# B and C of pairs 4 to 11 turned by the DMA crossbar instead of by PE and two evacuations

**Chip, cores, metric.** One core of a Trainium2 chip. The metric is the device time of one launch in microseconds (us). Engines: PE is TensorE (PEld its weight loads), DVE VectorE, ACT ScalarE, POOL GpSimd, SP SyncE, which here only issues DMAs.

## The reference, cut to what matters

A chunked state-space layer feeds a gated feed-forward layer. Cut:

```python
# x (4, 8, 768, 32), a (4, 8, 768), B and C (4, 8, 768, 16); float32
for c in range(nc):                       # chunks of 32 in the reference
    CB = einsum('bhin,bhjn->bhij', Cc, Bc)          # needs B and C with n on the contracted axis
    y_intra = einsum('bhij,bhjd->bhid', CB * L, xc)
    y_inter = einsum('bhin,bhnd->bhid', Cc, state) * decay_to_i
    state = decay_full * state + sum_j(Bc xc decay_from_j)
# then, per token: (relu(y @ w_gate) * (y @ w_val)) @ w_out, widths 256, 1536, 256
```

Tokens arrive on the partitions. The kernel's matmuls contract over the partitions, so B and C have to be turned before CB and y_inter; the state needs B unturned.

## The kernel before: the parts that matter

Work is cut into 12 pairs of 128-token chunks and 6 blocks of 512 tokens of the feed-forward layer. Block b carries the attention work of P = 2b+2 and Q = 2b+3 between its matmuls. The kernel keeps each engine's instructions in program order (its helper `in_order`). `inter(p)` is the first PE work that reads CT, `G(p)` the first that reads BT; `fout` is the feed-forward layer's last product.

```python
def transp(p, k, apart=False):                     # PE, into PSUM
    ...
    for i in range(2):
        nc.tensor.transpose(out=s["tp"][k][:, i], in_=s["tin"][k][i], identity=ident)

def tevac(p, beng, ceng):                          # BT: one copy; CT: two masked copies
    ...
    (beng.copy if beng is nc.scalar else beng.tensor_copy)(rows(BT), tokens(0))
    if ceng is nc.scalar:
        for t in range(2):
            nc.scalar.mul(rows(CT[:, t]), tokens(1), tmask[:, t:t + 1])
        return
    ...
for b in range(NBLK):
    P, Q, W = 2 * b + 2, 2 * b + 3, 2 * b + 1
    more = P < NPAIR
    for n in (P + 2, P + 3):                       # loads for the NEXT block, twelve DMAs on SP
        if n < NPAIR:
            load(n, nc.sync, nc.sync, nc.sync)
    ...                                            # gvh of f = 0..3; inter, Dm, yevac of W
    for f in range(4, NF):
        gv(b, f)
        if at("scale P", 4, 4, 4): scale(P, nc.gpsimd, nc.gpsimd)
        ...
        if at("turn P", 7, 6, 5):
            turn(P); tevac(P, nc.scalar, nc.vector)
        if at("turn Q", 99, 9, 8):
            turn(Q); tevac(Q, nc.scalar, nc.scalar)
    if more:
        inter(P, 0); inter(P, 1)                   # first reader of CT
    fout(b, 0); foevac(b, 0)
    if more:
        G(P); gevac(P)
    ...                                            # fout 1 and 2, Dm(P), G(Q), fout 3; outputs on SP
```

## Time and profile before

| | before |
|---|---|
| time | 135.2 us (135.13 to 136.19, 3 runs) |
| profiled run (136.74 us) | span 134.9 us, mean clock 0.987 |
| PE busy | 125.1 us (93%) |
| the 32 PE transposes that go | 0.22 us per four on the chain |

In the table of groups (line, engine, operation, tiles, shapes, count, busy us, mean ns of one, idle time before them) these are the ones that the change removes in part:

```profile
L318 PE MATMUL tp<-ident,bs 128*128 128x128 bf16 x44 | 4.4, 219 | 0.0
...
L338 ACT COPY BT<-tp 128x256 bf16<-128x256 bf16 x10 | 3.8, 376 | 0.5
...
L341 ACT ACTIVATE CT<-tp,tmask 128x256 bf16<-128x256 bf16 x8 | 3.4, 479 | 0.0
```

One PE transpose has a duration of 219 ns, but in a row they are pipelined: four advance the chain by 0.22 us. The chain, not the duration, is what a removed instruction gives back. The other lines of this profile are in the prediction.

### The profile page before, as it was taken

What the parts mean: (1) busy time and instruction counts of PE and PEld (TensorE: products, weight loads), DVE (VectorE), ACT (ScalarE), POOL (GpSimd) and SP (SyncE); (2) the same over time, 40 slices, a digit from 0 to 9 for tenths busy, and PEclk for the clock granted to TensorE, in tenths of its full rate; (3) what the DMA queues carried; (4) which work ended last, traced back from release to release, by engine and by line L of the source; (5) the groups of instructions that cost most, each with busy time, mean ns of one, the idle gap of its engine ahead of it and who ended that gap; (6) DMA issues with size and microseconds to landing.
All of it is one profiled execution on the core that took longest, in us unless ns stands there. A gap on an engine that the chain in (4) does not pass through costs nothing.

```text
span 134.9 us, 3130 instructions
## 1 busy us (share of the span) xinstructions
PE 125.1 (93%) x1150; PEld 82.7 (61%) x1157; DVE 90.7 (67%) x195; ACT 81.9 (61%) x177; POOL 37.8 (28%) x76
## 2 busy tenths in 40 slices
PE   6995398999999999999999999999999999999990
PEld 2444156555878656778557786567785577864780
DVE  5796086778637897657867568965588675687611
ACT  4075066547477776468784478764687845887410
POOL 7066063720209200248000293002480002200000
PEclk9999869999999999999999999999999999999999
DMA  3999999999423699028991239780220002200022
GB/s 70 190 151 192 211 187 135 201 190 104 44 78 96 77 119 102 3 83 149 121 114 10 78 87 120 90 99 3 83 78 0 0 0 83 78 0 0 5 80 76
DMA packets 68991, 12.10 MB, mean 90 GB/s; under 512 B 62768, under 2 KB 68976, under 8 KB 68976
## 3 DMA queue, kind: packets, MB, share of 16 engines
q1 hardware_dynamic: 62896, 8.88, 44.2%
q0 software_dynamic: 3184, 2.36, 11.7%
q10 hardware_dynamic: 2896, 0.66, 2.7%
q8 instruction: 9, 0.15, 0.5%
q14 instruction: 6, 0.05, 0.1%
HBM read 11.11 MB, written 3.15 MB: 106 GB/s over the span
## 4 chain that ended last, share of the span: by engine, by line
PE 57%; DVE 1%; issue 0%; DVEq 0%
PE o L490 19%; PE val L463 11%; PE gv L478 11%; PE gate L460 10%; PE y L435 2%; PE g L361 2%; PE A_ps L398 1%; PE tp L318 1%; PE y L424 1%; DVE h L467 0%; DVE ob L503 0%; DVEq L503 0%
## 5 line engine op out<-in xcount | busy, mean ns | idle before, releaser
L467 DVE TENSOR_TENSOR h<-r,val 128x512 bf16<-128x512 bf16 x48 | 32.6, 686 | 9.7 <-ACT r L466 8.8
L490 PE MATMUL o<-wo,h 128*128 128x256 bf16 x288 | 35.0, 273 | 0.1
L466 ACT ACTIVATE r<-gate 128x512 bf16<-128x512 f32 x48 | 28.3, 601 | 8.5 <-PE gate L460 6.2
L369 POOL TENSOR_SCALAR_AFFINE_SELECT gs<-gs 128x512 bf16<-128x512 bf16 (+1 forms) x24 | 12.4, 540 | 69.7 <-ACT gs L380 69.7
L490 PEld LDWEIGHTS <-h 128*128 128x128 bf16 x288 | 27.4, 98 | 5.1 <-issue 1.3
L463 PE MATMUL val<-yT,wv 128*128 128x512 bf16 x96 | 28.6, 379 | 0.3
L460 PE MATMUL gate<-yT,wg 128*128 128x512 bf16 x90 | 27.3, 379 | 0.3 <-ACT r L466 0.3
L482 DVE TENSOR_TENSOR h<-r,gv 128x256 bf16<-128x256 bf16 x48 | 20.0, 421 | 11.1 <-ACT r L481 10.5
L386 DVE TENSOR_TENSOR gs<-g,maskUT 128x512 bf16<-128x512 f32 x24 | 15.4, 686 | 12.9 <-issue 11.8
L481 ACT ACTIVATE r<-gv 128x256 bf16<-128x256 f32 x48 | 18.5, 385 | 6.6 <-PE gv L478 5.1
L478 PE MATMUL gv<-yT,wg 128*128 128x256 bf16 x96 | 18.8, 279 | 2.0 <-DMA wg<-in_moe_w_gate_dram 1.5
L478 PE MATMUL gv<-yT,wv 128*128 128x256 bf16 x96 | 19.0, 281 | 1.6 <-DMA wv<-in_moe_w_val_dram 1.6
L463 PEld LDWEIGHTS <-wv 128*128 128x128 bf16 x96 | 9.4, 98 | 11.3
L460 PEld LDWEIGHTS <-wg 128*128 128x128 bf16 x96 | 8.9, 98 | 7.1 <-issue 0.5
L380 ACT CAST gs<-g 128x512 bf16<-128x512 f32 x12 | 7.1, 589 | 9.2 <-PE g L361 9.0
L448 ACT CAST yT<-y 128x512 bf16<-128x512 f32 x12 | 7.0, 586 | 8.1 <-PE y L435 6.7
L478 PEld LDWEIGHTS <-wg 128*128 128x128 bf16 x96 | 9.1, 99 | 4.3 <-DMA wg<-in_moe_w_gate_dram 1.7
L478 PEld LDWEIGHTS <-wv 128*128 128x128 bf16 x96 | 9.5, 100 | 3.2 <-DMA wv<-in_moe_w_val_dram 1.9
L264 POOL TENSOR_TENSOR bs<-bcr,scaleBC 128x256 bf16<-128x256 f32 x16 | 9.6, 624 | 0.0
L506 ACT COPY ob<-o 128x512 f32<-128x512 f32 x10 | 5.9, 586 | 4.7 <-PE o L490 4.7
L406 DVE TENSOR_TENSOR Sm<-A_ps,smask 128x256 bf16<-128x256 f32 x20 | 8.3, 417 | 0.0
L163 PE MATMUL w<-warm 128*128 128x512 bf16 x18 | 6.2, 491 | 1.4 <-DVE bcr L81 1.3
(75 smaller groups left out, 110.8 us busy)
## 6 DMA issues: line engine op xcount, KB each, us to landing
out_dram<-ob SPq DMA_DIRECT2D x10, 256.0 KB, 2.2
xr<-in_x_dram SPq DMA_DIRECT2D x17, 128.0 KB, 3.8
bcr<-in_B_dram SPq DMA_DIRECT2D x16, 64.0 KB, 3.6
bcr<-in_C_dram SPq DMA_DIRECT2D x16, 64.0 KB, 3.4
xr<-in_x_dram SPq DMA_DIRECT2D x3, 256.0 KB, 7.3
wg<-in_moe_w_gate_dram POOLq DMA_DIRECT2D x3, 256.0 KB, 6.2
wv<-in_moe_w_val_dram POOLq DMA_DIRECT2D x3, 256.0 KB, 7.3
wo<-in_moe_w_out_dram POOLq DMA_DIRECT2D x1, 768.0 KB, 9.5
```

The source lines that it names most:

```text
L264: eng.tensor_tensor(out=bs.rearrange("s k (q t n) -> s k t q n", q=4, t=2)[:, :, t], in0=src[:, :, t], in1=f[:, :, 4 * t:4 * t + 4].to_bro ...
L369: nc.gpsimd.affine_select(out=dst, in_=dst, pattern=[[0, n], [1, 128]], compare_op=ALU.is_ge, fill=0.0, base=0, channel_multiplier=-1)
L386: nc.vector.tensor_tensor(out=d[:, q], in0=g[q], in1=m, op=ALU.mult)
L406: nc.vector.tensor_tensor(out=n, in0=A_ps, in1=smask, op=ALU.mult)
L460: nc.tensor.matmul(out=g, lhsT=wg[:, k, fs], rhs=yT[:, k, tk], start=(k == 0), stop=(k == 1))
L463: nc.tensor.matmul(out=v, lhsT=wv[:, k, fs], rhs=yT[:, k, tk], start=(k == 0), stop=(k == 1))
L466: nc.scalar.activation(r, g, AF.Relu)
L467: nc.vector.tensor_tensor(out=fst[b][:, f], in0=r, in1=v, op=ALU.mult)
L478: nc.tensor.matmul(out=gv_[:, j], lhsT=w[:, k, fs], rhs=yT[:, k, tk], start=(k == 0), stop=(k == 1), skip_group_check=True)
L481: nc.scalar.activation(r, gv_[:, 0], AF.Relu)
L482: nc.vector.tensor_tensor(out=fst[b][:, f, u * 256:(u + 1) * 256], in0=r, in1=gv_[:, 1], op=ALU.mult)
L490: nc.tensor.matmul(out=o[:, ts % 2], lhsT=fst[b][:, f, ts * 128:(ts + 1) * 128], rhs=wo[:, f], start=(f == 0), stop=(f == NF - 1), skip_gr ...
```

## The change

Intent: PE is the bound, so take the turns off it, and off ACT and DVE which empty them. POOL writes B and C, scaled, into a token-major tile with C in two copies that have zeros in the other half's columns (so no masking is needed later); one DMA through the crossbar (`dma_start_transpose`, which transposes on the way) turns all six 128x128 squares into SBUF.

```diff
+    def scale_turn(p):
+        ...
+        w = bc[p % NBC]                       # 3 buffers of [128, 6, 128], zeroed once
+        for j in range(2):
+            for t in range(2):
+                k = 2 * (1 + t) if j else 0
+                nc.gpsimd.tensor_tensor(out=w[:, k:k + 2]...[:, :, t], in0=..., in1=..., op=ALU.mult)
+        T = att.tile([128, 6, 128], BF16, tag="T", name="T")
+        nc.sync.dma_start_transpose(out=T, in_=w.rearrange("s k r -> s (k r)"))
+        s["B"] = [w[:, i] for i in range(2)]
+        s["BT"] = T[:, 0:2]
+        s["CT"] = T[:, 2:6].rearrange("r (t i) m -> r t i m", t=2)
+        cast_x(p, nc.gpsimd)
 ...
+            if b > 0 and more and f == 4:
+                scale_turn(P)
+                scale_turn(Q)
-            if at("turn P", 7, 6, 5):
+            if b == 0 and f == 7:
                 turn(P)
                 tevac(P, nc.scalar, nc.vector)
 ...
-            if at("turn Q", 99, 9, 8):
-                turn(Q)
-                tevac(Q, nc.scalar, nc.scalar)
```

Cut: the zeroing of `bc` on POOL in block 0, and the conditions that keep block 0 as it was. The loads stay at the head of each block.

More of the change, by code (lines that the diff above doesn't have):

```diff
@@ L251, in scale @@
         cast_x(p, ceng)
+    NBC = 3
+    bc = [const.tile([128, 6, 128], BF16, name="bc%d" % k) for k in range(NBC)]
+    def scale_turn(p):
+        b, c0 = p // PPB, 2 * (p % PPB)
+        s = st[p]
+        w = bc[p % NBC]
+        f = scaleBC[:, b, c0:c0 + 2].rearrange("s c j h -> s c (j h)")
+        for j in range(2):
+            for t in range(2):
+                k = 2 * (1 + t) if j else 0
+                nc.gpsimd.tensor_tensor(
+                    out=w[:, k:k + 2].rearrange("s i (q t n) -> s i t q n", q=4, t=2)[:, :, t],
+                    in0=s["bcr"][:, :, j, 4 * t:4 * t + 4],
+                    in1=f[:, :, 8 * j + 4 * t:8 * j + 4 * t + 4].to_broadcast([128, 2, 4, N]),
+                    op=ALU.mult)
+        T = att.tile([128, 6, 128], BF16, tag="T", name="T")
[4 more added lines that the diff above has]
+        cast_x(p, nc.gpsimd)
     def scale_bc(p, eng):
@@ L582 @@
                 decay()
-            if at("scale P", 4, 4, 4):
+            if b == 0 and f == 6:
+                for w in bc:
+                    nc.gpsimd.memset(w, 0.0)
+            if b == 0 and f == 4:
                 scale(P, nc.gpsimd, nc.gpsimd)
-            if at("scale Q", 8, 5, 4):
+            if b == 0 and f == 8:
                 scale(Q, nc.gpsimd, nc.gpsimd)
-            if at("turn P", 7, 6, 5):
+            if b > 0 and more and f == 4:
+                scale_turn(P)
+                scale_turn(Q)
+            if b == 0 and f == 7:
                 turn(P)
```

## The prediction

> **What bounds the kernel now.** I read the page's first two parts, then the chain that ended last in order of time, then the groups by line, then the issues of the sync engine's DMA queue (SP) as a timeline, then the table of stretches with the DMA share.
>
> ```profile
> PE 125.1 (93%) x1150; PEld 82.7 (61%) x1157; DVE 90.7 (67%) x195; ACT 81.9 (61%) x177; POOL 37.8 (28%) x76
> ...
> PE   6995398999999999999999999999999999999990
> ...
> PEclk9999869999999999999999999999999999999999
> ```
>
> TensorE (PE) is busy 93% of the span; from slice 7 (about 24 us) on every slice is full. A busy PE need not be the bound, so the chain is asked next. From 53.5 us on it is PE alone, piece touching piece, until the last evacuation. Here is the end of block 2 (b=2), from its second turn on:
>
> ```profile
> 68.52 0.22 PE tp L318 x4
> 68.74 0.43 PE gate L460 x2
> 69.17 0.43 PE val L463 x2
> 69.61 0.11 PE A_ps L398
> 69.71 0.43 PE gate L460 x2
> 70.15 0.43 PE val L463 x2
> 70.58 0.43 PE gate L460 x2
> 71.01 0.43 PE val L463 x2
> 71.44 0.11 PE y L424 x2
> 71.55 1.41 PE o L490 x12
> ```
>
> The columns are start, length, what. A turn of one pair (four transposes, L318) takes 0.22 us of this chain and nothing waits for it. The y piece of L424 is the first reader of CT on PE: `inter(P)`. So PE in program order is the bound, the other engines have slack, and the only direct gain is PE time.
>
> **What the Trainium skill says.** (1) "VectorE: DVE Perf Modes", section "The three transpose paths": a 128x128 bf16 transpose is given as 390 ns on TensorE and 1309 ns by the DMA crossbar, the latter into SBUF. This trace has 219 ns for one PE transpose and, in a row, 0.22 us for four; it has no crossbar transfer. (2) "Advanced Engine Details and Errata", section "X-Bar Transpose (TRN2)": such DMAs are said to be as fast as regular ones. That contradicts (1) for one of 196 KB unless (1) is nearly all fixed cost; no run yet tells. (3) "DMA: Bandwidth & Descriptors", section "Queues, rings and completion order": on each DMA engine the descriptors of one issuer's ring are consumed in order, so a transfer issued last starts last. The trace agrees as far as it goes: SP issues in program order and the last of a burst of loads lands when the burst has drained. (4) "TensorE: Matmul & The Clock Gate", section "Part 1": about 3.4 us of idleness halves the PE clock, and about as much work restores it. The trace agrees: PE is nearly idle from 13 to 16 us, then the granted clock is 0.50 in three successive stretches of 1 us and 0.83 in the next.
>
> **The change part by part.**
>
> *Removed on PE.* Pairs 4 to 11 lose their turns: 8 x 4 transposes. In the chain each turn is 0.22 us, so 8 x 0.22 = 1.76 us, 0.44 us in each of blocks 1 to 4. The end follows in full, if nothing else waits: 135.2 - 1.8 = 133.4 us.
>
> *Removed on ACT and DVE.* BT copies of pairs 4 to 11: 8 x 375 ns; CT of the P pairs on DVE: 4 x 685 ns; CT of the Q pairs on ACT: 8 x 479 ns. That is 6.8 us of ACT and 2.7 us of DVE, none of it on the chain. PE was held by ACT in the gate group for 0.3 us in all, so I count 0.
>
> *Added on POOL.* Each pair has four multiplies of 128x128 in place of two of 128x256 (624 ns). Taking the length to grow with the elements plus a small fixed part, I estimate 360 ns each, so 1.44 us for 1.25 us per pair. POOL idles for 10 us per block (its causal masks wait 69.7 us in total for ACT), so 0. The three memsets of the padded tiles, estimated at 0.85 us each from the 568 ns of the 128x512 memset, fall between the two scales of block 0: the second scale ended at 27.9 us and would end at about 30.4, and its turn comes at 35.1. Again 0.
>
> *Moved, and this decides it.* The turned C is now ready when a DMA lands. The instruction order of the changed kernel on SP has, in each of blocks 1, 2 and 3: twelve loads for the next block, then the transpose of P, the transpose of Q, then the outputs. POOL has its inputs scaled early (about 4 us after the block's start), but the transposes stand in the SP queue behind loads that are not needed until the next block. When does SP get there? In the kernel before, the twelve loads of block 2 are these (start and length of issue, first and last):
>
> ```profile
> 60.83 0.42 SPq L109 DMA_DIRECT2D xr<-in_x_dram  x1
> ...
> 68.87 0.58 SPq L111 DMA_DIRECT2D bcr<-in_C_dram  x1
> ```
>
> They cannot start earlier, because the outputs of the block before stand ahead of them and wait for ACT. The last issue ends at 69.45 us, where `inter(P)` starts at 71.44. And the rings are still full then (columns: stretch, length, busy time and count of PE, PEld, DVE, ACT and POOL, the clock, the DMA share, GB/s):
>
> ```profile
> 69.00:70.00 1.00, 1.00 (x7) 0.51 (x6) 0.44 (x1) 1.00 (x4) 0.00 (x0) 1.00 1.20 134
> 70.00:71.00 1.00, 1.00 (x6) 0.47 (x5) 0.59 (x1) 0.87 (x2) 0.00 (x0) 1.00 1.44 103
> 71.00:72.00 1.00, 1.00 (x11) 0.76 (x9) 1.00 (x4) 0.60 (x1) 0.00 (x0) 1.00 0.08 6
> ```
>
> The loads drain at about 71.1 us. The same views give a last issue at 52.2 and a drain near 53.9 in block 1, and 89.3 and 91.0 in block 3. Counted from the blocks' starts (first gv piece at 40.8, 59.7 and 78.3), the drains are at 13.1, 11.4 and 12.7 us. `inter(P)` stood at 11.7 and comes at 11.3 without the two turns. So PE is already waiting by 1.8, 0.1 and 1.4 us (3.3 us in all) when the first byte of the transpose can move; then come the transfer and its completion.
>
> How long is that? The tile is 128x768 bf16, 196 KB, six squares. Three estimates. As a regular DMA: the 256 KB outputs land 2.2 us after issue, so about 2 us. By (1), scaled by six: 7.9 us, surely too much if part of the 1309 ns is fixed. By short pieces: the loads move 1024 runs of 64 or 128 bytes each, one load per 0.72 us or so; a transpose that must write runs of 32 bytes would write 6144 and so take some 4 us. I choose 3.5 us after the drain. The stall is then 3.3 + 3 x 3.5 = 13.8 us in blocks 1 to 3. Block 4 has no loads: its transposes go out when POOL is done, about 3 to 5 us into the block, with 7 us in hand, so 0 there.
>
> *The clock.* A stall of 3.5 to 5.3 us idles PE long enough for the clock to fall, in some blocks and not in all. At half speed for about 3.2 us, as at 16 to 19 us, PE loses 1.6 us; I count 3 us for the three blocks.
>
> *Q.* Its transpose follows P's by one transfer. `G(Q)` comes 5.0 us after `inter(P)` (76.47 less 71.44), which covers any transfer under 5 us: 0.
>
> *Sum.* 135.2 - 1.8 + 13.8 + 3 = 150.2, so 150 us, 11% slower.
>
> **The rivals.** *Hidden transfer:* the loads leave earlier or the crossbar overtakes them, nothing waits, and 133.4 us results, "same" by the 2% rule and a little better in truth. For it: POOL could feed the transpose 7 us ahead of need, and DMA is idle in half of the slices. Against it: the SP order, and the drain times above, at or after the need even with a transfer of zero length. *Fast crossbar:* 2 us after the drain, stalls of 3.8, 2.1 and 3.4 us, little or no loss of clock, so about 143 to 145 us. *Slow crossbar:* 7.9 us each. Then P stalls by 3.3 + 23.7 = 27 us, Q adds up to 3 us a block (less where PE is at half clock), and the clock costs 5 us: 166 to 174 us. A slow issue on SP would look the same. *Relief of ACT or DVE as a gain beyond PE's:* the chain has no such waits to give back, so under 0.5 us.
>
> **Range and chances.** Most weight lies between the fast crossbar and some way towards the slow one: 141 to 164. To be within 2% the three stalls together must stay under 4.5 us, while 3.3 us of that is there before a byte moves; I give this 6%. To be over 2% faster needs more than the whole PE saving, 2%. Slower: 92%.
>
> **What would show it.** If right, the chain of the profile after holds three waits of PE on the DMA of T, of 3 to 6 us, ahead of y of L424 (its line is moved by 25 in the changed file) in blocks 1, 2 and 3, and none in block 4, whose length shrinks by about 0.44 us; SP shows the transposes after the twelfth load; the granted clock dips to about 0.5 after at least one stall; blocks 0 and 5 keep their lengths. If the transposes are issued right at POOL's end, or PE waits nowhere for T, the central step is wrong. If the waits are there but of another length, the size of the crossbar's time is what failed. Waits ahead of `G(Q)` would mean a transfer of over 5 us.

## The result, and the profile after

The changed kernel takes 143.3 us (median of 4 runs, 141.32 to 144.17), the kernel before in the same rounds 135.28 us (135.13 to 136.19). A ratio here is the mean time of one kernel's fast runs over that of the other's of the same rounds, so not quite the ratio of the medians: 1.0529, interval 1.041 to 1.0648. Slower by 5%, where 11% was forecast.

The profiled run is the slowest (144.17 us) and counts as slow, being over 1.5% above the fastest. So what is read from it is checked below against runs of equal clock. From its page: PE's busy time and, in 40 slices, PE and the granted clock.

```profile
PE 126.7 (89%) x1118; PEld 82.6 (58%) x1125; DVE 88.8 (62%) x191; ACT 76.7 (54%) x161; POOL 41.9 (29%) x95
...
PE   6999689999999946999995999955999999999990
...
PEclk9999869999999996899999999999999999999999
```

PE was full from slice 7 on; now it has three holes, and the clock dips once after the first of them. What the holes wait for, from PE's rows of the waits (engine, line, releaser: us in total, times, longest) and PE's timeline (start, length, what, and idle time before it):

```profile
PE y L449 <- DMA T<-bc: 8.2, 3, 3.2
```

```profile
54.75 0.61 PE L449 MATMUL y<-T,Sm 128*128 128x128 bf16 x4 [3.23 <-DMA T<-bc]
...
76.48 0.28 PE L449 MATMUL y<-T,Sm 128*128 128x128 bf16 x2 [1.96 <-DMA T<-bc]
...
97.62 0.40 PE L449 MATMUL y<-T,Sm 128*128 128x128 bf16 x4 [3.01 <-DMA T<-bc]
```

Exactly three waits, all at `inter(P)`, in blocks 1, 2 and 3; block 4 has none. The SP queue's timeline shows why T is late. In each block the last of twelve loads and the transposes behind it:

```profile
50.61 0.58 SPq L111 DMA_DIRECT2D bcr<-in_C_dram  x1
51.29 2.83 SPq L272 DMA_TRANSPOSE T<-bc  x2
...
72.52 1.00 SPq L111 DMA_DIRECT2D bcr<-in_C_dram  x1
73.62 2.56 SPq L272 DMA_TRANSPOSE T<-bc  x2
...
92.59 2.11 SPq L111 DMA_DIRECT2D bcr<-in_C_dram  x1
94.81 2.58 SPq L272 DMA_TRANSPOSE T<-bc  x2
```

P's transpose lands 3.4, 2.8 and 2.8 us after SP takes it up, and PE's reader starts within 0.05 us of that. POOL is not late: in this trace its multiplies for P and Q are through at 44.0, 67.1 and 87.2 us, 6.5 to 7.6 us before SP takes the transposes up. The dip, in stretches of 1 us (stretch, length, busy us and count of PE, PEld, DVE, ACT and POOL, the clock, DMA share, GB/s):

```profile
54.00:55.00 1.00, 0.25 (x3) 0.26 (x4) 0.00 (x0) 0.00 (x0) 0.00 (x0) 0.82 0.89 173
55.00:56.00 1.00, 1.00 (x8) 0.76 (x6) 0.00 (x0) 0.00 (x0) 0.00 (x0) 0.50 0.12 24
56.00:57.00 1.00, 1.00 (x6) 0.75 (x5) 0.00 (x0) 0.00 (x0) 0.00 (x0) 0.50 0.00 0
57.00:58.00 1.00, 1.00 (x9) 0.45 (x11) 0.00 (x0) 0.00 (x0) 0.00 (x0) 0.50 0.00 0
58.00:59.00 1.00, 1.00 (x15) 0.68 (x8) 0.52 (x1) 0.59 (x2) 0.00 (x0) 0.97 0.00 0
```

A trace cut into blocks is the cleanest comparison, since the start of a run varies. Block lengths in us, from the first `gvh` matmul of one block to that of the next (the last to the span's end, so to 0.1 us), each from the profiled run's PE timeline:

| kernel | 0 | 1 | 2 | 3 | 4 | 5 |
|---|---|---|---|---|---|---|
| before | 26.61 | 18.78 | 18.61 | 18.51 | 18.40 | 19.9 |
| changed | 26.54 | 23.01 | 20.19 | 21.25 | 17.95 | 20.0 |
| e1, transposes first | 25.48 | 18.07 | 18.06 | 18.07 | 17.95 | 20.1 |
| e2, no turn at all | 27.01 | 18.06 | 18.06 | 18.07 | 17.95 | 19.9 |

Block 4 of the changed kernel is 0.45 us shorter than before, the other three are longer.

### The profile page after: what moved, and what is told of

Read it like the earlier page. It is cut to its first block, busy times and chain, and to the rows that moved or that the text cites. A ratio compares the mean times of both kernels' runs of the same rounds, so it can differ in the third digit from the quotient of the medians.

```text
span 142.5 us, 3079 instructions
## 1 busy us (share of the span) xinstructions
PE 126.7 (89%) x1118; PEld 82.6 (58%) x1125; DVE 88.8 (62%) x191; ACT 76.7 (54%) x161; POOL 41.9 (29%) x95
## 3 DMA queue, kind: packets, MB, share of 16 engines
q0 software_dynamic: 3184, 2.36, 11.4%
## 4 chain that ended last, share of the span: by engine, by line
PE 50%; SPq 19%; DMA 17%; issue 5%; ACT 3%; DVE 2%; POOL 1%; ACTq 0%; DVEq 0%; POOLq 0%
PE o L515 19%; SPq L111 14%; PE gv L503 8%; PE val L488 7%; PE gate L485 7%; DMA T<-bc 6%; SPq L109 5%; DMA wv<-in_moe_w_val_dram 4%; DMA bcr<-in_B_dram 4%; DMA out_dram<-ob 2%; PE g L386 2%; PE y L460 2%; PE y L449 2%; DVE gs L411 1%; PE A_ps L423 1%
## 5 line engine op out<-in xcount | busy, mean ns | idle before, releaser
L515 PE MATMUL o<-wo,h 128*128 128x256 bf16 x288 | 36.0, 279 | 0.0
L491 ACT ACTIVATE r<-gate 128x512 bf16<-128x512 f32 x48 | 28.7, 599 | 12.2 <-PE gate L485 11.2
L515 PEld LDWEIGHTS <-h 128*128 128x128 bf16 x288 | 28.1, 100 | 5.0 <-issue 1.3
L266 POOL TENSOR_TENSOR bc<-bcr,scaleBC 128x128 bf16<-128x128 f32 x32 | 11.9, 403 | 0.0
L449 PE MATMUL y<-T,Sm 128*128 128x128 bf16 x28 | 3.1, 232 | 8.2 <-DMA T<-bc 8.2
L449 PEld LDWEIGHTS <-Sm 128*128 128x128 bf16 x40 | 3.2, 107 | 10.5 <-DMA T<-bc 9.7
```

Of the source, the lines that this page charges most:

```text
L266: nc.gpsimd.tensor_tensor(out=w[:, k:k + 2].rearrange("s i (q t n) -> s i t q n", q=4, t=2)[:, :, t], in0=s["bcr"][:, :, j, 4 * t:4 * t + ...
L491: nc.scalar.activation(r, g, AF.Relu)
L515: nc.tensor.matmul(out=o[:, ts % 2], lhsT=fst[b][:, f, ts * 128:(ts + 1) * 128], rhs=wo[:, f], start=(f == 0), stop=(f == NF - 1), skip_gr ...
```

## The experiments

The theory (A): the transposes stand in SP's queue behind twelve loads that nobody needs before the next block. Rivals: (B) the crossbar transfer, or its traffic, is itself the cost wherever it stands; (C) POOL makes its input late. Then the two sizes, of the transfer and of the clock's dip, were asked.

**e1: the loads behind the transposes.**

```diff
-        for n in (P + 2, P + 3): ...load(n, ...)          # at the head of every block
+        if b == 0: (the same)                             # block 0 alone
 ...
             if b > 0 and more and f == 4:
                 scale_turn(P)
                 scale_turn(Q)
+                for n in (P + 2, P + 3): ...load(n, ...)
```

> The changed kernel with one move: in blocks 1 to 3 the twelve loads for the next block are issued after the two crossbar transposes and no longer before them. Theory A (the transposes stand in the sync engine's queue behind loads that nobody needs yet): no wait of PE on T in any block, no dip of the clock after block 0, 133.0 to 134.0 us (before less 1.76 us of PE time). Rival B (the crossbar transfer or its traffic beside PE and the loads is itself what costs): the waits on T stay at over 1 us each in blocks 1 to 3 and the time stays above 138 us. Rival C (POOL makes the transposes' input late): as B, with SP seen waiting for POOL up to the need of T.

Measured: correct, 133.62 us (133.25 to 134.98), ratio to before 0.9885 (0.9812 to 0.9957). No wait on T. SP in block 2 of this kernel, and PE's first reader of T there:

```profile
58.14 0.38 SPq L532 DMA_DIRECT2D out_dram<-ob  x1
59.41 3.20 SPq L272 DMA_TRANSPOSE T<-bc  x2
62.67 0.57 SPq L109 DMA_DIRECT2D xr<-in_x_dram  x1
...
72.59 3.99 SPq L532 DMA_DIRECT2D out_dram<-ob  x2
```

```profile
68.61 0.28 PE L449 MATMUL y<-T,Sm 128*128 128x128 bf16 x2
```

The reader has no idle time before it and starts 6 us after both transposes are issued. The same instructions and the same bytes, in another order on one queue, take the whole loss away. B and C both fall.

**e2: no turn at all** (a wrong result on purpose).

```diff
-        T = att.tile([128, 6, 128], BF16, tag="T", name="T")
-        nc.sync.dma_start_transpose(out=T, in_=w.rearrange("s k r -> s (k r)"))
+        T = Tfix                                          # one zeroed tile for all
```

> Wrong result on purpose: the transposes are left out and one zeroed tile stands in for every T, so that the turned operands cost nothing at all. It measures the removed work alone. If the removed PE time is the only gain: 133.0 to 134.0 us (135.3 less 1.76), blocks 1 to 4 shorter by 0.44 us each. If the relief of ACT and DVE, or fewer waits elsewhere, were worth more: under 132.8 us. If the saving is taken back by another wait of PE: over 134.5 us.

Measured: wrong as meant, 134.2 us (133.0 to 135.39, 16 runs), ratio 0.9861 (0.9833 to 0.989). Its blocks 1 to 4 are those of e1 to 0.01 us (table above): once its order is right, the crossbar costs nothing in these blocks, and e1 has the whole gain that this change can give. The sum of the four savings is 2.16 us, where 1.76 was forecast; blocks 3 and 4 give the 0.44 us each, blocks 1 and 2 give 0.72 and 0.55.

**e3: only Q by the crossbar**, P by PE as before, loads still first.

```diff
             if b > 0 and more and f == 4:
-                scale_turn(P)
+                scale(P, nc.gpsimd, nc.gpsimd)
                 scale_turn(Q)
+            if b > 0 and at("turn P", 7, 6, 5):
+                turn(P); tevac(P, nc.scalar, nc.vector)
```

> The changed kernel with P's turn back on PE (and its two evacuations) in all blocks; only the Q pairs go through the crossbar, still behind the loads. G(Q) comes 5 us after inter(P). Theory A: a T that lands some 3 us after the loads' last issue is in time for Q, so no wait on T, half of the PE saving: 134.2 to 134.8 us. Rival B (crossbar traffic itself disturbs): a wait of PE on T of over 1 us per block, or other instructions lengthened, over 136 us.

Measured: correct, 134.57 us (133.48 to 135.73, 20 runs), ratio 0.9893 (0.9863 to 0.9922), no wait of PE on T. The very position in the queue that makes P late is in time for Q, whose first reader `G(Q)` stands 5 us further down PE's program: T landed 2.1, 2.9 and 1.9 us before it in blocks 1 to 3. So not the transposes' place alone but place against deadline counts.

**e4: the transposes on ACT's queue**, loads unchanged on SP.

```diff
-        nc.sync.dma_start_transpose(out=T, in_=...)
+        nc.scalar.dma_start_transpose(out=T, in_=...)
```

> The changed kernel with the two transposes issued from ACT's queue, in ACT's program order after the relu of f=4, the loads unchanged on SP. The DMA engines are as full of load traffic as before, but the transposes no longer stand behind all twelve loads in issue. Theory A (order of issue is what counts): T lands about 8 us into the block, no wait on T, 133.2 to 135 us, the upper end if each issue holds ACT for over a microsecond. Rival B (the 16 DMA engines, filled by loads, are the bound, whoever issues): T lands at about the same time as in the changed kernel and the time stays over 140 us.

Measured: correct, 138.67 us (137.72 to 140.11), ratio 1.0201 (1.0136 to 1.0265). There is no wait on T, so A stands here as well: among full load traffic it landed 4.8 us (median) after its issue and that was early enough. But the time missed the forecast by nearly 4 us. ACT's and PE's timelines in block 1:

```profile
44.13 2.69 ACTq L272 DMA_TRANSPOSE T<-bc  x2
46.92 1.57 ACT L491 ACTIVATE r<-gate 128x512 bf16<-128x512 f32 x3 [2.25 <-PE gate L485]
```

```profile
47.56 0.59 PE L488 MATMUL val<-yT,wv 128*128 128x512 bf16 x2 [0.94 <-ACT r L491]
```

The two issues hold ACT for 2.7 us. The relu that would free a PSUM bank comes late, and PE waits in each of the four blocks: PE's waits for this relu are 3.5 us in all, of the 4.2 us by which blocks 1 to 4 are longer than e1's; the rest is not accounted for. (The wait's label on the relu says PE; the relu's operand had long been there, and what ended its idle time was ACT's own queue.) An issue of a transpose is not free for the engine that does it.

**e5: dummy matmuls in the stall.**

```diff
         if more:
+            if 1 <= b <= 3:
+                keep_warm(9)                              # 9 matmuls of 512 columns
             inter(P, 0)
```

> The changed kernel with nine dummy matmuls of 512 columns (9 x 0.216 = 1.9 us of PE time at full clock) on PE just before inter(P) in blocks 1 to 3, where PE otherwise waits 3.2, 2.0 and 3.0 us for T. If the three waits are set by T's landing alone, the dummies fit into them: the end does not move later, the remaining waits shrink to about 1.3, 0 to 0.2 and 1.1 us, and the clock is never halved in them; so every run sits where the changed kernel's run of clock 1.000 sits, 141 to 142 us, about 1 to 1.5 us under the changed kernel's median. If T were not what PE waits for (or the dip of the clock were only a bystander), the dummies would add up to 3 x 1.9 us: 145 to 149 us.

Measured: correct, 143.71 us (142.15 to 144.75), ratio 1.0483 (1.0403 to 1.0563), against the changed kernel's 1.0529. The waits on T shrank from 8.2 to 3.5 us while 5.8 us of work was put in, and in the profiled run the clock stayed at 1.000, block 1 falling from 23.01 to 21.59 us. So most of the dummies fit into the stall, as A says. But the end did not come earlier, as I had expected: blocks 2 and 3 became 0.3 and 0.7 us longer. T landed 3.0 and 3.5 us after its issue there and not 2.8 and 2.8, and in block 2 its issue came 0.2 us later too. The two runs at a clock of 1.000, 142.15 and 142.88 us, lie above the changed kernel's one such run, 141.32. The verdict on the whole time is inconclusive.

**e6: useful work in the stall.**

```diff
+        fout(b, 0)
         if more:
             inter(P, 0)
             inter(P, 1)
-        fout(b, 0)
```

> The changed kernel with fout(b,0), 12 matmuls worth 1.31 us, moved from behind inter(P) to ahead of it, so that useful work stands in the stall; loads and transposes stay in their order. Theory A (three waits for a T that lands at a fixed time): each wait shrinks by 1.3 us, no dip, total about 143.3 - 3 x 1.3 - 1 = 138 to 139 us. Rival (the loss is not in these waits but spread, by traffic or by a slower clock): no gain to speak of, 142 to 144 us.

Measured: correct, 140.06 us (138.68 to 144.06, 5 runs), ratio 1.0318 (1.0242 to 1.0394): 2.1 points below the changed kernel, less than the 3 to 4 expected. The waits are still 2.1, 1.4 and 2.4 us: in the profiled runs T landed 0.2, 0.8 and 0.7 us later in its block than in the changed kernel, and 1.31 us less these is what each wait shrank by. The profiled run (a slow one) shows a halved clock at the end of the wait of 2.1 us in block 1:

```profile
55.00:56.00 1.00, 0.00 (x0) 0.00 (x0) 0.00 (x0) 0.00 (x0) 0.00 (x0) 1.00 1.09 164
56.00:57.00 1.00, 0.04 (x1) 0.04 (x2) 0.00 (x0) 0.00 (x0) 0.00 (x0) 0.94 0.64 125
57.00:58.00 1.00, 1.00 (x12) 0.44 (x12) 0.00 (x0) 0.00 (x0) 0.00 (x0) 0.50 0.77 147
```

**e7: each transpose cut in two**, C's four squares, then B's two.

```diff
-        nc.sync.dma_start_transpose(out=T, in_=w...)
+        for k0, k1 in ((2, 6), (0, 2)):
+            nc.sync.dma_start_transpose(out=T[:, k0:k1], in_=w[:, k0:k1]...)
```

> The changed kernel with each transpose cut in two: the four squares of C first (inter(P) needs only these), then the two of B. It measures how the crossbar's time depends on size. If the 1.22 us that SP spends on one transpose is proportional to its size and the rest of the 2.8 us to landing is fixed, C takes 0.8 us of SP and lands after 2.4 us, B takes 0.4: each of the three waits shrinks by 0.4 us and the time is 1 to 1.5 us below the changed kernel, 142 us. If the time to landing is fixed whatever the size: no change of the first wait, landing at 2.7 us, within 0.5 us of the changed kernel. If it is the data that takes the time behind the loads (my forecast, 3.5 us after the drain for 196 KB): waits shorter by a third, over 1 us each, under 140.5 us.

Measured: correct, 146.23 us (141.79 to 146.66); one run is fast, three are slow with a mean clock of 0.962, so there is no ratio. It answers the question of size. The transposes of the changed kernel (SP's time for one, min/median/max in ns; then us from issue to landing), and of e7:

```profile
L272 SPq DMA_TRANSPOSE T<-bc x8: 1211/1223/1503, 51.3 to 108.5; - x8
...
DMA to landing us min/median/max: 2.7/2.8/3.5
```

```profile
L273 SPq DMA_TRANSPOSE T<-bc x16: 1189/1239/1637, 51.0 to 112.8; - x16
...
DMA to landing us min/median/max: 2.3/2.4/4.1
```

SP spends 1.2 us on a transpose of two, four or six squares alike. The twelve of e7 that are not the first of their block land after 2.3 to 2.5 us whether they have two squares or four (but for one at 2.7 and one at 4.1, both with an instruction fetch in flight, of which more below), against 2.7 to 2.8 as a rule with six: nearly all of the time is fixed. The first of a block, C of P, was through 2.9, 2.7 and 3.1 us after issue in blocks 1 to 3, and the waits (3.2, 1.8 and 3.0 us) did not shrink. The extra issues show no cost of their own: blocks 1, 2 and 4 of the profiled run are within 0.2 us of the changed kernel's. Block 3 is 2.8 us longer, with the clock at half for 6.8 us where the changed kernel kept it full. Why the clock fell in three of the four runs more than in the changed kernel stays open.

**e8 and e9: the best version, and its control.** The runs of most versions lie in two clusters. Block 0 waits for the first weights, and the clock is halved there in some runs. e8 is e1 with eight dummy matmuls ahead of block 0; e9 is the kernel before with the same line.

```diff
+    keep_warm(8)
     for b in range(NBLK):
```

> The version with the loads behind the transposes, and eight dummy matmuls (1.7 us) ahead of block 0, where PE waits for the first weights and the clock is halved for about 3 us in part of the runs of every version. If that halving explains why the runs of one kernel lie in two clusters about 1 us apart: no halving, all runs in the lower cluster, 133.0 to 133.8 us. If the clusters have another cause: two clusters as before, 133.2 and 134.9. If the dummies delay the start: over 134.5 in all runs.

> The kernel before with nothing of the change, only the eight dummy matmuls ahead of block 0 that the best version has. It separates the two gains of that version. If the dummies do nothing but keep the clock up: all runs at a clock near 1.000 and at the lower cluster of the kernel before, 134.9 to 135.4 us, a ratio of 0.993 to 0.997, so that of the best version's 2.0% some 1.4% belong to the crossbar. If the dummies bring all of it: under 134 us. If they bring nothing: two clusters as before, median about 136.

Measured: e8 correct, 133.29 us (132.75 to 133.44, 4 runs), ratio 0.9797 (0.9748 to 0.9846), all at a clock of 0.999 or 1.000. e9 correct, 135.43 us (134.79 to 135.85, 14 runs), all of them at a clock of 0.993 or more, ratio 0.9989 (0.9962 to 1.0016). In the rounds of e9, the unchanged kernel's ten runs at such a clock had a median of 135.05 us and the nine others 136.08. So the clusters are the clock's, about 1 us apart; the dummies remove the upper cluster and cost some 0.4 us of the lower one, which comes to nothing for the mean. Between the medians of e9 and e8, both with a full clock though of separate rounds and chips, lie 2.1 us: that is the crossbar in its right place, and it agrees with the 2.15 us that e1's blocks 1 to 4 are shorter than those before. By the 2% rule e1, e2, e3 and e9 count as "same" and e4 and e8 as "unclear"; the intervals of e1, e2, e3 and e8 lie below 1 all the same.

## Why the prediction was right and wrong

The direction, the mechanism and the place were right; the size was about twice what was measured, 14.8 us forecast and 8.0 us found between the medians.

**PE's saving, 1.76 us:** right, slightly low. With nothing in the way (e2) it is 2.16 us. The turns are 1.78 us of that by the trace; the other 0.36 lies in `fout`'s matmuls of blocks 1 and 2, and its cause was not looked for.

**ACT, DVE and POOL count 0:** right in effect. POOL's multiply took 403 ns and not 360, its three memsets 2.1 us together and not 2.6; neither e1 nor e2 shows a new wait of PE from them.

**The loads stand ahead, three waits and none in block 4:** right. The transposes follow the twelfth load, PE waits at `inter(P)` in blocks 1 to 3, and e1 removes all of it by order alone. The waits, forecast as 3 to 6 us, were 3.2, 2.0 and 3.0. SP took up the transposes 11.2, 10.5 and 11.5 us into the blocks, where the profile of before had the last issue ending at 11.4, 9.9 and 11.1. (I read the starts of blocks 2 and 3 off the chain, as 59.7 and 78.3; the timeline has 59.55 and 78.16, which makes the 3.3 us of waiting before the drain 3.6.)

**The transfer, "I choose 3.5 us after the drain":** this is the step that failed. The drain itself was about right: 1.7 us after the last issue forecast, 1.9, 1.5 and 1.5 measured (the last packets of the loads in the trace end at 53.07, 74.98 and 96.22 us). From there to landing it took 1.6, 1.5 and 1.4 us and not 3.5. So T landed 3.4, 2.8 and 2.8 us after SP took it up, where 5.2 was meant, and the three waits come to 8.2 us and not 13.8. Two errors lie in it. I set the drain, the transfer and its completion one after the other, though a fixed part of the transfer runs while the loads drain: with no load ahead (e1, blocks 2 and 3) T's first packet leaves 1.18 us after the issue, and behind the loads it left after 1.48, 1.20 and 1.22. What makes T late is thus the 9 to 10 us that SP spends issuing twelve loads; their bytes, still in flight, delayed its landing by at most 0.7 us over the usual 2.7. And I let size weigh, in the estimates of 4 and of 7.9 us between which and 2 us I chose; e7 shows that three times the squares add some 0.4 us, and the trace has 768 packets of 256 bytes for one transpose and not 6144 runs of 32.

In block 4, with no loads ahead, P's took 3.5 us. There the trace shows an instruction fetch of 16 KB (queue q8) in flight from 107.41 to 108.37 us. Over all profiled runs, the first transpose of a block with six squares and no loads ahead landed after 3.4 to 4.0 us in the six cases with such a fetch in flight, and after 2.7 to 2.8 in the seven without. That the fetch is the cause was not tested.

The lowest estimate, taken from the 2.2 us of the outputs in the trace of before, was the near one, and still too long. The "fast crossbar" rival, 143 to 145 us, was the case that happened.

**The clock, 3 us:** too much, for the same reason. In the profiled run the clock dipped after one of the three waits. Block 1 is 4.94 us longer than in e1, of which 3.23 is the wait; blocks 2 and 3 exceed their waits by 0.16 and 0.18, so the dip cost about 1.5 us. The changed kernel's run of clock 1.000, at 141.32 us, has no dip. It stands 6.2 us above the 135.1 us of the unchanged kernel's runs at full clock, and the waits less the saving make 8.2 - 2.2 = 6.0. So the waits account for it, in fast runs too.

**Q, 0:** right; `G(Q)` waits for no transfer, and e3 shows Q in time even so placed.

## What to carry to other kernels

A queue that issues in program order makes the urgent transfer wait for every bulk prefetch written above it: place a DMA with a deadline in this iteration ahead of loads for the next, and look at each reader's deadline in PE's program, since the same place was late for P and in time for Q. When sizing a DMA wait, separate the fixed part, which overlaps with what is ahead in the queue, from the part that grows with bytes. Which engine issues matters as well: 1.2 us of issue was free on SP and cost PE time on ACT.

## What the Trainium skill lacked or had wrong

- "DMA: Bandwidth & Descriptors", section "Issuing engines are not separate DMA queues", calls the sequencer's time to initiate a DMA "usually small relative to the DMA itself". For a crossbar transpose from SBUF it is 1.2 us of the 2.3 to 2.8 us to landing, for two, four or six squares alike; on ACT it delayed the relu and PE lost 3.5 us to waits for it (e4).
- "VectorE: DVE Perf Modes", section "The three transpose paths", gives 1309 ns for one square by the crossbar and does not tell the fixed part from the part that grows with size. Here six squares in one DMA landed 2.7 to 2.8 us after issue, two or four squares after 2.3 to 2.5. The statement of "Advanced Engine Details and Errata", section "X-Bar Transpose (TRN2)", that they are as fast as regular DMAs is nearer: 196 KB turned in 2.8 us, though 256 KB of output were stored in 2.2.
- "TensorE: Matmul & The Clock Gate", section "Part 1", puts the fall of the clock at an idle window of about 3.4 us. It was halved at the end of waits of 3.23 us (changed kernel, block 1), 2.96 (e7, block 3) and 2.10 us (e6, block 1), and 1.2 us after the end of one of 3.18 (e7, block 1); it was not after 3.01 (changed kernel, block 3) and 2.39 (e6, block 3). The length of a wait alone did not tell.
- No page warns that a transfer with a near deadline is held up by loads that are issued ahead of it on the same engine's queue; here that was 8.2 us of PE waits.
- No page gives what an instruction fetch costs a transfer that is in flight with it: 0.7 to 1.2 us more to landing went with one here, as told above.
